# Attention scores of the first query block on one Trainium2 core: three f32r products in place of one f32 product

## The chip, the core and the metric

The kernel runs on one core of a Trainium2 chip. The metric is the device time of one execution in microseconds (us). Of the kernel before, three timed runs are known; a fourth execution was profiled. Engines are named as the profile names them: PE is TensorE (its matmuls), PEld is TensorE's weight loads, DVE is VectorE, ACT is ScalarE, POOL is GpSimd, SP is SyncE, which here only issues transfers.

## What is computed

Block-causal attention over 8 batches of 8 heads, 576 positions of 64 features, followed by a gated MLP over all 4608 tokens:

```python
scores = scale * np.matmul(q, k.transpose(0, 1, 3, 2))     # 576 x 576 for each of 64 heads
mask = block_i >= block_j                                   # blocks of 64 positions
scores = np.where(mask, scores, -1000000000.0)
...
attn = np.exp(scores)                                       # after the row maximum is taken off
attn = attn / (np.sum(attn, axis=-1, keepdims=True) + 1e-09)
return np.matmul(attn, v).astype(np.float32)
...
gate = 1.0 / (1.0 + np.exp(-(x @ w_gate)))
val = x @ w_val
return (gate * val @ w_out).astype(np.float32)
```

x is the attention's output with 512 features; w_gate and w_val are 512 x 1536, w_out is 1536 x 512.

## The kernel before

**Pairs.** Two heads make a pair, so there are 32 pairs. The 64 features of head 0 lie on partitions 0 to 63 and those of head 1 on partitions 64 to 127. KQ holds a pair's transposed keys (KQ[:, 0]) and queries (KQ[:, 1]), 576 columns each. The queries are cut into four blocks of 128 (block 0 to block 3) and a tail of 64; block i needs only the first 128(i+1) keys.

**Halves.** From pair 4 on (the constant REST_FROM), most score products are not taken from KQ itself. Keys and scaled queries are rounded to f32r (KH, QH) and what the rounding took off is rounded too (KL, QL). Three f32r products QH·KH, QL·KH and QH·KL add up to the score in PSUM. Five steps make the operands, in the function `prep_steps`: ACT writes KH ("ks", L395) and QH ("qs", L400), POOL writes KL ("kl", L405; DVE does it at L407 in the front), DVE writes QL ("ql", L409), and POOL copies the tail's queries into QBH and QBL ("qx", L415). A sixth step, "pm" (L402), has POOL multiply the 128 query columns of block 0 in KQ by the scale, in place: block 0 alone is still one f32 product of KQ with KQ, so it needs no halves, and QH and QL hold only the 448 columns behind it.

**Scores.** The function `scores` makes one block's products, for both heads. The two heads use different rows of PE's array (64 rows each, `tile_position`), so their matmuls run at the same time, and the profile shows them in twos. Block 3 has a PSUM tile of its own, block 2 too, and blocks 1 and 0 share one: block 1 in columns 0 to 255, block 0 in columns 256 to 383. In that third tile all three products of block 1 come first and the f32 product of block 0 stands last. An f32 matmul is two passes on PE, and the profile lists both.

**Order of the work.** Pairs 0 to 7 are laid out in a hand-written list (FRONT), which fixes the order of every instruction on every engine; this is the front, about the first 131 us. Pairs 8 to 31 run in a loop whose steps are listed in REST; between the steps the matmuls of the first third of the MLP (L179, L188) are dealt out to PE, so that PE has work while softmax and the transposes of other pairs run. On POOL a loop turn holds, in this order, DMA issues that move blocks of exponentials (L621), XL (L844), four copies into G (L615), the issue of rb (L292: the reciprocal sums, spread over the partitions), then pm and kl of the next pair, the issue of r_d (L292, it waits for rT of DVE at L568) and qx. The division L703 on DVE needs rb; it frees the PSUM tile that the scores of a later block are written to. From about 545 us on only the rest of the MLP runs (L1341, L1411).

Of the kernel before, what the change touches and what calls it, by code (L numbers as in the profile page):

```python
# [48 lines left out]
c2a.3@ rc.3 d2.c4 xh.1@ t3b.3 rD.3 pm.4 S10.4 t3a.3 c3b.3 tlb.3 x0.2 x1.2 dH.c3 S3.4 ms10.4@ c3a.3 tla.3 clb.3 pm.5  # L49
# [7 lines left out]
ldq.7 d4.o0 c3.5 h.10 tt5.5 h.11 tl.5 pm.6 ql.6 ldva.5@ d3.c7 h.12 cta.5 kl.6 ctb.5 ldq.8 d4.c7 t2.5 ldvb.5 dH.c6 cl.5  # L57
# [3 lines left out]
AV0.5 qs.7 gt.2 f.o2 st.4 AV1.5 ks.7 ext.6 d4.o1 c2.6 ldvb.7 ql.7 x0.5 sq.o2 ldvc.7 t3.6 h.23 d5.o1 ldvc.8 rc.6 pm.7  # L61
tl.6 kl.7 x1.5 ldq.9 qx.7 St.7 pa.o1 c3.6 dH.o1 cl.6 tt5.6 gm.2 gl.1@ dL.o1 dk.8 h.24 h.25 h.26 f.o3@ rD.6 cta.6 mxt.7
ext.7 d1.o2 d2.o2 ctb.6 ldva.8@ S2.7 S3.7 st.5 ms3.7@ ms2.7@ S10.7 d3.o2 d4.o2 d5.o2 gh.2 sq.o3 xl.4@ ldvb.8 h.27
mx2.7 gt.3 pm.8 h.28 pa.o2 h.29 h.30 ms10.7@ rB.6 dH.o2 gl.2 h.31 mx3.7 ldk.9 e2a.7 mx0.7 dL.o2 e2b.7 mx1.7 e3a.7 gm.3
# [9 lines left out]
def attn_glu_kernel(ctx: ExitStack, tc: tile.TileContext, q, k, v, w_gate, w_val, w_out, out):  # L74
    nc = tc.nc
# [152 lines left out]
    with ExitStack() as s2:  # L228
# [9 lines left out]
        KS, QS = [at.tile([P, S], F32R, name=f"K{e}") for e in "HL"], [at.tile([P, S - P], F32R, name=f"Q{e}") for e in "HL"]  # L238
# [99 lines left out]
        def mark(engine, ins):  # L338
            last[engine] = ins.ins
# [39 lines left out]
        def rows(h):  # L379
            return slice(64 * h, 64 * h + 64)  # L380

        def prep_steps(p):

            KQ = cv.tile([P, 2, S], F32, name="KQ", bufs=2)

            def step(what, alt=False):
                if what in ("dk", "dq"):
                    i = "kq".index(what[1])
                    turn = last.get("DVE")
                    ins = nc.vector.transpose(out=KQ[:, i], in_=rqks[p % 2][:, i])  # L390
                    for other in maxima or [turn] * bool(turn):
                        behind(ins.ins, other)
                    mark("DVE", pin("DVE", ins))
                elif what == "ks":
                    ins = nc.scalar.copy(out=KS[0], in_=KQ[:, 0])  # L395
                    for other in exps:
                        behind(ins.ins, other)
                    mark("ACT", pin("ACT", ins))
                elif what == "qs":
                    mark("ACT", pin("ACT", nc.scalar.mul(out=QS[0], in_=KQ[:, 1, P:], mul=scale)))  # L400
                elif what == "pm":
                    chain("POOL", pin("POOL", nc.gpsimd.tensor_scalar_mul(KQ[:, 1, :P], KQ[:, 1, :P], scale)))  # L402
                elif what == "kl":
                    if alt:
                        chain("POOL", pin("POOL", nc.gpsimd.tensor_sub(out=KS[1], in0=KQ[:, 0], in1=KS[0].bitcast(F32))))  # L405
                    else:
                        mark("DVE", pin("DVE", nc.vector.tensor_sub(out=KS[1], in0=KQ[:, 0], in1=KS[0].bitcast(F32))))  # L407
                elif what == "ql":
                    chain("DVE", pin("DVE", nc.vector.scalar_tensor_tensor(  # L409
                        out=QS[1], in0=KQ[:, 1, P:], scalar=scale, in1=QS[0].bitcast(F32), op0=ALU.mult,  # L410
                        op1=ALU.subtract)))
                elif what == "qx":
                    for x, src in zip(QBS, QS):
                        for h in range(2):
                            chain("POOL", pin("POOL", nc.gpsimd.tensor_copy(out=x[rows(h), h], in_=src[rows(h), S - P - D:])))  # L415
                state[p] = KQ, None, VSs[p % 3]

            return step

        def prep(p):  # L420

            step = prep_steps(p)
            for part in (("dk", "dq", "ks", "qs", "pm", "kl"), ("ql",), ("qx",)):
                for what in part:
                    step(what, what == "kl")
                yield

        def attend(p):
# [38 lines left out]
            def scores(ps, i, c):  # L467


                n = P * (i + 1)  # L470
                q = slice(i * P, (i + 1) * P)
                ops = [(KQ[:, 1, q], KQ[:, 0, :n])]
                if rest and i:
                    q = slice((i - 1) * P, i * P)
                    ops = [(QS[a][:, q], KS[b][:, :n]) for a, b in ((0, 0), (1, 0), (0, 1))]
                for k, (x, y) in enumerate(ops):
                    for h in range(2):
                        matmul(ps[:, h, c:c + n], lhsT=x[rows(h)], rhs=y[rows(h)], start=(k == 0),
                               stop=(k == len(ops) - 1), tile_position=(64 * h, 0))
                        if h == k == 0:  # L480
                            first_mm[:] = pe_last
# [21 lines left out]
            def s_blocks(*groups):  # L503
# [4 lines left out]
                for k, (ps, group) in enumerate(zip(tiles, groups)):  # L508
                    for j, i in enumerate(group):
                        scores(ps, i, 2 * P * j)  # L510
                        if rest and dealt and k == j == 0:
                            behind(first_mm[0], dealt[-1])
# [204 lines left out]
            def fine(what, alt=False, queue=nc.sync):  # L717

                i, h = what[1:2], "ab".find(what[-1])
                if what[0] == "S":  # L720
                    group = (1, 0) if i == "1" else () if i == "t" else (int(i),)
                    ps = keep["S" + i] = two_banks()
                    for j, c in enumerate(group):
                        scores(ps, c, 2 * P * j)
# [843 lines left out]
```

## Time and profile before

| | us |
|---|---|
| three timed runs | 1096.95, 1099.28, 1099.80 |
| their median | 1099.28 |
| the profiled execution, its own time | 1099.69 |
| span of the profiled execution | 1097.8 |

The span is the time from the first to the last recorded instruction on the core; the execution's own time also holds what lies around it (1.89 us). Instructions of a matmul overlap, since each is recorded until its last result is written: the distance from one start to the next says what one costs, its duration does not.

### The profile page before, as it was taken

The numbers are of one execution on the slowest core, as the hardware profiler recorded it, in microseconds if no ns is written. First come the engines' busy times: TensorE is split into PE (matmuls) and PEld (weight loads), VectorE is DVE, ScalarE is ACT, GpSimd is POOL, SyncE is SP. The second block draws the span as 40 slices with busy tenths as digits, with TensorE's granted clock in tenths as the row PEclk, the third lists the DMA queues.
The fourth block names the chain that finished last, engine by engine and source line by source line (L and its number), as shares of the span: only waits on it lengthen the run. The fifth ranks groups of instructions, "written<-read, shape, count | busy, mean of one in ns | idle before, by whom it ended". The sixth has DMA issues, their size and how long they took to land.

```text
span 1097.8 us, 19466 instructions
## 1 busy us (share of the span) xinstructions
PE 1080.7 (98%) x6593; PEld 929.5 (85%) x6593; DVE 862.1 (79%) x1488; ACT 602.7 (55%) x1321; POOL 532.3 (48%) x692
## 2 busy tenths in 40 slices
PE   8899999999999999999999999999999999999998
PEld 6577777778787778778899999999999999999997
DVE  6899999898989898787699768578785585665744
ACT  6887777777787777643353444534454142341421
POOL 3655499898989898710113030321305336243340
PEclk9999999999999999999999999999999999999999
DMA  8797599899888887745033362350886517345251
GB/s 162 162 206 159 128 184 190 187 189 197 185 194 177 200 175 184 198 122 170 22 97 103 123 221 78 144 187 34 293 296 230 188 50 224 103 128 186 74 164 58
DMA packets 264619, 174.87 MB, mean 159 GB/s; under 512 B 200988, under 2 KB 222092, under 8 KB 263880
## 3 DMA queue, kind: packets, MB, share of 16 engines
q1 hardware_dynamic: 247000, 148.54, 50.6%
q0 software_dynamic: 7008, 17.68, 6.9%
q10 hardware_dynamic: 10512, 7.41, 2.3%
q8 instruction: 52, 0.85, 0.3%
q14 instruction: 47, 0.39, 0.1%
HBM read 104.73 MB, written 47.60 MB: 139 GB/s over the span
## 4 chain that ended last, share of the span: by engine, by line
PE 83%; DVE 4%; DMA 4%; ACT 3%; POOL 2%; issue 2%; SPq 1%; ACTq 0%; DVEq 0%; POOLq 0%
PE b L1341 32%; PE m L1411 12%; PE bank L358 11%; PE m L179 10%; PE m L188 7%; PE b L1411 7%; PE bank L179 3%; SPq L292 1%; DMA rqk<-in_q_dram 1%; DMA rqk<-in_k_dram 1%; DMA rb<-r_d 1%; PE bank L188 1%; POOL G L615 1%; PE bank L363 1%; ACT XB L499 1%
## 5 line engine op out<-in xcount | busy, mean ns | idle before, releaser
L1341 PE MATMUL b<-XH,w 128*128 128x384 f32 x1344 | 349.0, 335 | 0.0
L1341 PEld LDWEIGHTS b<-XH,w 128*128 128x128 f32 x1344 | 243.8, 188 | 3.6
L1341 PE MATMUL b<-XL,w 128*128 128x384 f32 x672 | 223.5, 335 | 0.0
L1136 POOL TENSOR_TENSOR XB<-XB 128x384 f32<-128x384 f32 x20 | 21.5, 1076 | 238.0 <-DMA XB<-xT_d 238.0
L1341 PEld LDWEIGHTS b<-XL,w 128*128 128x128 f32 x672 | 126.1, 188 | 1.7
L1411 PE MATMUL m<-wo,hH 128*128 128x512 f32 x368 | 119.9, 391 | 0.0
L358 PE MATMUL bank<-G,VS 128*64 128x64 f32 (+3 forms) x1264 | 95.0, 305 | 2.6 <-POOL G L615 1.5
L358 PEld LDWEIGHTS bank<-G,VS 128*64 128x64 f32 x1264 | 64.6, 137 | 35.1 <-issue 7.6
L1364 ACT ACTIVATE g<-g 128x384 f32<-128x384 f32 x72 | 37.8, 525 | 93.1 <-DVE g L1377 49.3
L1149 ACT CAST XH<-XB 128x1536 fp32r<-128x1536 f32 (+2 forms) x72 | 65.1, 941 | 35.7 <-DVE XB L1147 27.3
L188 PE MATMUL m<-wo,hH 128*128 128x512 f32 x256 | 83.8, 393 | 0.0
L179 PE MATMUL m<-XH,wg 128*128 128x512 f32 x240 | 81.2, 394 | 0.4 <-ACT t L203 0.4
L179 PE MATMUL m<-XH,wv 128*128 128x512 f32 x240 | 81.2, 395 | 0.0
L1411 PEld LDWEIGHTS m<-wo,hH 128*128 128x128 f32 x368 | 69.0, 188 | 12.9
L487 DVE TENSOR_REDUCE nm<-bank 128x2 f32<-128x1024 f32 (+1 forms) x96 | 76.9, 801 | 2.2 <-ACT Z L499 0.6
L1150 DVE TENSOR_TENSOR XL<-XB,XH 128x1536 fp32r<-128x1536 f32 (+2 forms) x72 | 75.8, 1085 | 0.0
L1411 PE MATMUL m<-wo,hL 128*128 128x512 f32 x184 | 72.1, 392 | 0.0
L1411 PE MATMUL b<-wo,hH 128*128 128x512 f32 (+1 forms) x216 | 71.4, 383 | 0.0
L1405 POOL TENSOR_TENSOR pr<-pr,pr 128x512 f32<-128x512 f32 x33 | 42.6, 1296 | 42.6 <-DMA pr<-part_d 29.6
L499 ACT ACTIVATE Z<-bank,nm 128x512 f32<-128x512 f32 (+3 forms) x104 | 53.5, 529 | 7.8 <-DVE nm L487 4.5
L188 PEld LDWEIGHTS m<-wo,hH 128*128 128x128 f32 x256 | 47.9, 188 | 9.9 <-issue 0.2
L1349 POOL TENSOR_TENSOR hL<-v,hH 128x384 fp32r<-128x384 f32 x36 | 38.9, 1094 | 33.0 <-ACT hH L1348 30.3
(219 smaller groups left out, 2626.3 us busy)
## 6 DMA issues: line engine op xcount, KB each, us to landing
pr<-part_d SPq DMA_DIRECT2D x66, 256.0 KB
XB<-xT_d SPq DMA_DIRECT2D x16, 576.0 KB
part_d<-pr SPq DMA_DIRECT2D x36, 256.0 KB
rqk<-in_q_dram SPq DMA_DIRECT2D x120, 72.0 KB
rqk<-in_k_dram SPq DMA_DIRECT2D x120, 72.0 KB
out_dram<-pr SPq DMA_DIRECT2D x33, 256.0 KB
wgv_d<-st SPq DMA_DIRECT2D x8, 896.0 KB
w<-wgv_d SPq DMA_DIRECT2D x4, 1792.0 KB
```

The source lines that it names most:

```text
L179: mm = nc.tensor.matmul(ps, lhsT=lh, rhs=rh, start=(i == 0), stop=(i == n - 1))
L188: mm = nc.tensor.matmul(ps, lhsT=lh[:, f, t * P:(t + 1) * P], rhs=rh, start=(f == i == 0), stop=(f == F1 - 1 and i == 2))
L358: pe_last[:] = [pin("PE", nc.tensor.matmul(*args, **kw)).ins]
L487: mark("DVE", nc.vector.tensor_reduce(out=nm_()[:, c0:c0 + 2], in_=ps[:, :, c:c + n], axis=AX.X, op=ALU.max, negate=True))
L499: mark("ACT", nc.scalar.activation(out=dst, in_=src, func=AF.Exp, bias=nm_()[:, c0 + h:c0 + h + 1], accum_out=sm[:, 5 * h + i:5 * h + i + 1]))
L1149: nc.scalar.copy(out=XO[j][0][:, a:b], in_=x)
L1150: sub = nc.vector.tensor_sub(out=XO[j][1][:, a:b], in0=x, in1=XO[j][0][:, a:b].bitcast(F32))
L1341: mm = nc.tensor.matmul(ps, lhsT=lh, rhs=rh, start=(first and k == 0), stop=(k == n - 1), skip_group_check=not first)
L1349: (nc.vector if q else nc.gpsimd).tensor_sub(out=hL[:, f, n:n + N2], in0=h, in1=hH[:, f, n:n + N2].bitcast(F32))
L1364: mark2("ACT", nc.scalar.activation(out=t, in_=c, func=AF.Tanh, scale=0.5))
L1405: nc.gpsimd.tensor_add(out=pr[t], in0=pr[t], in1=other)
L1411: mm = nc.tensor.matmul(po[t][:, cols], lhsT=lh[:, f, t * P:(t + 1) * P], rhs=wo[:, f, e, cols], start=((whole or half == 0) and i == 0), ...
```

## The change

Block 0 is now made from the halves like the other blocks. QH and QL have 576 columns (448 before), so "qs" on ACT and "ql" on DVE run over all queries; "pm" is gone from POOL, in the loop and five times from the front's list. `scores` takes several blocks and goes through them product by product: QH·KH of block 1, QH·KH of block 0, QL·KH of block 1, QL·KH of block 0, and so on. Only block 1's first product opens the PSUM bank (`start`).

```diff
-c2a.3@ rc.3 d2.c4 xh.1@ t3b.3 rD.3 pm.4 S10.4 t3a.3 c3b.3 tlb.3 x0.2 x1.2 dH.c3 S3.4 ms10.4@ c3a.3 tla.3 clb.3 pm.5
+c2a.3@ rc.3 d2.c4 xh.1@ t3b.3 rD.3 S10.4 t3a.3 c3b.3 tlb.3 x0.2 x1.2 dH.c3 S3.4 ms10.4@ c3a.3 tla.3 clb.3 
...
-        KS, QS = [at.tile([P, S], F32R, name=f"K{e}") for e in "HL"], [at.tile([P, S - P], F32R, name=f"Q{e}") for e in "HL"]
+        KS, QS = [at.tile([P, S], F32R, name=f"K{e}") for e in "HL"], [at.tile([P, S], F32R, name=f"Q{e}") for e in "HL"]
...
-                    mark("ACT", pin("ACT", nc.scalar.mul(out=QS[0], in_=KQ[:, 1, P:], mul=scale)))
-                elif what == "pm":
-                    chain("POOL", pin("POOL", nc.gpsimd.tensor_scalar_mul(KQ[:, 1, :P], KQ[:, 1, :P], scale)))
+                    mark("ACT", pin("ACT", nc.scalar.mul(out=QS[0], in_=KQ[:, 1], mul=scale)))
...
-                        out=QS[1], in0=KQ[:, 1, P:], scalar=scale, in1=QS[0].bitcast(F32), op0=ALU.mult,
+                        out=QS[1], in0=KQ[:, 1], scalar=scale, in1=QS[0].bitcast(F32), op0=ALU.mult,
...
-            for part in (("dk", "dq", "ks", "qs", "pm", "kl"), ("ql",), ("qx",)):
+            for part in (("dk", "dq", "ks", "qs", "kl"), ("ql",), ("qx",)):
...
-            def scores(ps, i, c):
...
+            def scores(ps, *blocks):
+
+                todo = []
+                for i, c in blocks:
+                    n = P * (i + 1)
+                    q = slice(i * P, (i + 1) * P)
+                    ops = [(QS[a][:, q], KS[b][:, :n]) for a, b in ((0, 0), (1, 0), (0, 1))] if rest else \
+                        [(KQ[:, 1, q], KQ[:, 0, :n])]
+                    todo.append([(x, y, c, n, k == 0, k == len(ops) - 1) for k, (x, y) in enumerate(ops)])
+                for k, step in enumerate(zip(*todo)):
+                    for j, (x, y, c, n, start, stop) in enumerate(step):
+                        for h in range(2):
+                            matmul(ps[:, h, c:c + n], lhsT=x[rows(h)], rhs=y[rows(h)], start=start and j == 0, stop=stop,
+                                   tile_position=(64 * h, 0), skip_group_check=j > 0)
```

PE's instructions at the scores of one pair of the loop, from block 2's last product to the MLP's next matmul, stand before as follows (x2 is one for each head; the f32 product of KQ is one row here and two passes on PE):

```order
L358 MATMUL bank<-KL,QH 128x384 x2
L358 MATMUL bank<-KH,QH 128x256 x2
L358 MATMUL bank<-KH,QL 128x256 x2
L358 MATMUL bank<-KL,QH 128x256 x2
L358 MATMUL bank<-KQ 128x128 x2
L179 MATMUL m<-XL_435,wv_117 128x512
```

With the change the same place reads:

```order
L358 MATMUL bank<-KL,QH 128x384 x2
L358 MATMUL bank<-KH,QH 128x256 x2
L358 MATMUL bank<-KH,QH 128x128 x2
L358 MATMUL bank<-KH,QL 128x256 x2
L358 MATMUL bank<-KH,QL 128x128 x2
L358 MATMUL bank<-KL,QH 128x256 x2
L358 MATMUL bank<-KL,QH 128x128 x2
L179 MATMUL m<-XL_435,wv_117 128x512
```

The f32 product is gone, and a product of 128 columns stands behind each of block 1's; nothing else moved on PE here.

POOL's instructions of one loop turn, from the last issue of rb to the tail's copies, stand before as follows:

```order
L292 DMA rb<-r_d 64x512
L218 TENSOR_TENSOR hL<-h_2055,hH 128x512
L402 TENSOR_SCALAR KQ<-KQ 128x128
L405 TENSOR_TENSOR KL<-KQ,KH 128x576
L292 DMA r_d<-rT 4x32x32
L415 COPY QBH<-QH 64x64 x2
```

With the change (lines behind 402 are two lower):

```order
L292 DMA rb<-r_d 64x512
L218 TENSOR_TENSOR hL<-h_2079,hH 128x512
L403 TENSOR_TENSOR KL<-KQ,KH 128x576
L292 DMA r_d<-rT 4x32x32
L413 COPY QBH<-QH 64x64 x2
```

The scaling of KQ is gone from ahead of KL; the rest of the turn keeps its order.

## Rows read from the trace of the kernel before

**Rows 1.** The page's first part: busy us (share of the span) xinstructions.

```profile
span 1097.8 us, 19466 instructions
...
PE 1080.7 (98%) x6593; PEld 929.5 (85%) x6593; DVE 862.1 (79%) x1488; ACT 602.7 (55%) x1321; POOL 532.3 (48%) x692
```

**Rows 2.** Busy us by stretch: us, engines (xinstructions), granted clock, DMA share, GB/s.

```profile
50.00:100.00 50.00, 47.21 (x336) 35.62 (x335) 47.41 (x88) 42.74 (x111) 28.79 (x34) 1.00 0.83 182
...
200.00:250.00 50.00, 49.88 (x400) 39.65 (x400) 44.41 (x77) 37.64 (x90) 45.66 (x71) 1.00 0.93 186
...
350.00:400.00 50.00, 48.95 (x354) 39.04 (x354) 43.32 (x73) 38.60 (x100) 44.30 (x68) 1.00 0.87 191
```

**Rows 3.** Longest waits of PE, 131 to 545 us: us in total, times, longest us.

```profile
PE bank L358 <- DVE xT L703: 2.1, 5, 0.8
PE bank L358 <- POOL G L615: 1.5, 1, 1.5
PE bank L358 <- DVE QL L409: 0.7, 2, 0.4
```

**Rows 4.** PE in order of time, pair 15's blocks 1 and 0: start us, us, instruction.

```profile
218.47 0.38 PE L358 MATMUL bank<-KH,QH 64*128 64x256 f32 x2
218.66 0.31 PE L358 MATMUL bank<-KH,QL 64*128 64x256 f32 x2
218.78 0.31 PE L358 MATMUL bank<-KL,QH 64*128 64x256 f32 x2
218.90 0.41 PE L358 MATMUL bank<-KQ 64*128 64x128 f32 x4
219.24 0.50 PE L179 MATMUL m<-XL,wv 128*128 128x512 f32 x1
```

**Rows 5.** The same, from 219.20 us on: the second pass of KQ alone.

```profile
219.00 0.31 PE L358 MATMUL bank<-KQ 64*128 64x128 f32 x2
```

**Rows 6.** Weight loads of the same place, in order of time.

```profile
218.44 0.21 PEld L358 LDWEIGHTS bank<-KH,QH 64*128 64x128 f32 x2 [0.34 <-PE bank L358]
218.54 0.22 PEld L358 LDWEIGHTS bank<-KH,QL 64*128 64x128 f32 x2
```

**Rows 7.** PE in order of time in the front: f32r products, then another array layout.

```profile
54.24 0.33 PE L358 MATMUL bank<-KH,QL 64*128 64x384 f32 x2
54.41 0.34 PE L358 MATMUL bank<-KL,QH 64*128 64x384 f32 x2
54.68 0.44 PE L363 MATMUL m<-ident,Z 128*128 128x128 f32 x2
```

**Rows 8.** Line L402 (pm): count, duration ns min/median/max, first and last start.

```profile
L402 POOL TENSOR_SCALAR KQ<-KQ x28: 523/524/1185, 48.2 to 443.5; 128x128 f32<-128x128 f32 x28
```

**Rows 9.** POOL in order of time, pair 12's pm and kl.

```profile
172.15 0.52 POOL L402 TENSOR_SCALAR KQ<-KQ 128x128 f32<-128x128 f32 x1
172.67 1.40 POOL L405 TENSOR_TENSOR KL<-KQ,KH 128x576 fp32r<-128x576 f32 x1
```

**Rows 10.** DVE in order of time, pairs 11 (from 158 us) and 12 (from 173 us).

```profile
158.19 1.43 DVE L565 TENSOR_SCALAR sm<-sm 128x9 f32<-128x9 f32 x1
...
160.04 0.58 DVE L409 SCALAR_TENSOR_TENSOR QL<-KQ,QH 128x448 fp32r<-128x448 f32 x1
...
173.09 1.46 DVE L409 SCALAR_TENSOR_TENSOR QL<-KQ,QH 128x448 fp32r<-128x448 f32 x1
```

**Rows 11.** PE in order of time, its waits in pairs 11 to 13 and 27.

```profile
160.68 0.50 PE L358 MATMUL bank<-KH,QL 64*128 64x512 f32 x2 [0.26 <-DVE QL L409]
...
174.61 0.50 PE L358 MATMUL bank<-KH,QL 64*128 64x512 f32 x2 [0.44 <-DVE QL L409]
...
189.89 0.39 PE L358 MATMUL bank<-KH,QH 64*128 64x256 f32 x2 [0.35 <-DVE xT L703]
...
391.39 0.39 PE L358 MATMUL bank<-KH,QH 64*128 64x256 f32 x2 [0.27 <-DVE xT L703]
```

**Rows 12.** ACT in order of time, pair 11's QH.

```profile
157.39 0.60 ACT L400 ACTIVATE QH<-KQ 128x448 fp32r<-128x448 f32 x1
```

More of the change, by code (lines that the diff above doesn't have):

```diff
@@ L56 @@
 st.3 d4.c6 d1.c7 e0b.5 d3.o0 ks.6 d5.c6 AV0.4 pa.c6 e0a.5 AV1.4 ldva.7 x0.4 e1a.5 x1.4 gm.0 d2.c7 t3.5 qs.6 sq.c7
-ldq.7 d4.o0 c3.5 h.10 tt5.5 h.11 tl.5 pm.6 ql.6 ldva.5@ d3.c7 h.12 cta.5 kl.6 ctb.5 ldq.8 d4.c7 t2.5 ldvb.5 dH.c6 cl.5
+ldq.7 d4.o0 c3.5 h.10 tt5.5 h.11 tl.5 ql.6 ldva.5@ d3.c7 h.12 cta.5 kl.6 ctb.5 ldq.8 d4.c7 t2.5 ldvb.5 dH.c6 cl.5
 h.13 rc.5 gt.1 c2.5 d5.c7 qx.6 d5.o0 S2.6 pa.c7@ ms2.6@ rD.5 mx2.6 S3.6 sq.o1 S10.6 ms3.6@ h.14 dH.c7 h.15 xh.4
@@ L60 @@
 h.19 mx0.6 dL.o0@ d1.o1 rB.5 dk.7 e1b.6 gh.1 e3a.6 h.20 d2.o1 h.21 h.22 e1a.6 St.6 ldk.8 d3.o1 e0a.6 t2.6 e0b.6 mxt.6
-AV0.5 qs.7 gt.2 f.o2 st.4 AV1.5 ks.7 ext.6 d4.o1 c2.6 ldvb.7 ql.7 x0.5 sq.o2 ldvc.7 t3.6 h.23 d5.o1 ldvc.8 rc.6 pm.7
+AV0.5 qs.7 gt.2 f.o2 st.4 AV1.5 ks.7 ext.6 d4.o1 c2.6 ldvb.7 ql.7 x0.5 sq.o2 ldvc.7 t3.6 h.23 d5.o1 ldvc.8 rc.6
 tl.6 kl.7 x1.5 ldq.9 qx.7 St.7 pa.o1 c3.6 dH.o1 cl.6 tt5.6 gm.2 gl.1@ dL.o1 dk.8 h.24 h.25 h.26 f.o3@ rD.6 cta.6 mxt.7
 ext.7 d1.o2 d2.o2 ctb.6 ldva.8@ S2.7 S3.7 st.5 ms3.7@ ms2.7@ S10.7 d3.o2 d4.o2 d5.o2 gh.2 sq.o3 xl.4@ ldvb.8 h.27
-mx2.7 gt.3 pm.8 h.28 pa.o2 h.29 h.30 ms10.7@ rB.6 dH.o2 gl.2 h.31 mx3.7 ldk.9 e2a.7 mx0.7 dL.o2 e2b.7 mx1.7 e3a.7 gm.3
+mx2.7 gt.3 h.28 pa.o2 h.29 h.30 ms10.7@ rB.6 dH.o2 gl.2 h.31 mx3.7 ldk.9 e2a.7 mx0.7 dL.o2 e2b.7 mx1.7 e3a.7 gm.3
 e0b.7 d1.o3 d2.o3 xh.5 e1b.7 e3b.7 e1a.7 d3.o3 u.0 e0a.7 AV0.6 d4.o3 d5.o3 ldq.10 ldk.10 AV1.6 rc.7 ks.8 tt5.7 pa.o3@
@@ L414, in step @@
                         for h in range(2):
-                            chain("POOL", pin("POOL", nc.gpsimd.tensor_copy(out=x[rows(h), h], in_=src[rows(h), S - P - D:])))
+                            chain("POOL", pin("POOL", nc.gpsimd.tensor_copy(out=x[rows(h), h], in_=src[rows(h), S - D:])))
                 state[p] = KQ, None, VSs[p % 3]
@@ L465, in copy_out @@
                     mark("ACT", pin("ACT", nc.scalar.copy(out=dst, in_=src)))
-            def scores(ps, i, c):
[L470 to L481, printed above, removed]
+            def scores(ps, *blocks):
[11 more added lines that the diff above has]
+                                   tile_position=(64 * h, 0), skip_group_check=j > 0)
+                            if h == k == j == 0:
+                                first_mm[:] = pe_last
             def softmax(ps, i, c):
@@ L508, in s_blocks @@
                 for k, (ps, group) in enumerate(zip(tiles, groups)):
[L509 to L512, printed above, removed]
+                    scores(ps, *((i, 2 * P * j) for j, i in enumerate(group)))
+                    if rest and dealt and k == 0:
+                        behind(first_mm[0], dealt[-1])
                 if rest:
@@ L722, in fine @@
                     ps = keep["S" + i] = two_banks()
-                    for j, c in enumerate(group):
-                        scores(ps, c, 2 * P * j)
+                    if group:
+                        scores(ps, *((c, 2 * P * j) for j, c in enumerate(group)))
                     if not group:
```

## The prediction, made before the changed kernel was run

> **What bounds the kernel now.** I read the page's first part, then busy time by stretch, then PE's waits, then single places in order of time. In the first part PE is busy for 1080.7 of 1097.8 us [rows 1]. The stretches say where it is not the whole story: at 50 to 100 us PE idles 2.8 of 50 us while DVE is busy for 47.4; at 200 to 250 us it idles 0.12; at 350 to 400 us, 1.05, with POOL busy for 44.3 [rows 2]. [...] The waits behind the front give the names: 2.1 us in five places for xT (the division that frees a PSUM tile), 1.5 us once for a POOL copy into G, 0.7 us in two places for QL [rows 3]. So a pair of the loop costs what PE has to do, plus a few short waits on a chain in which POOL and DVE take turns. The change touches both: it gives PE more matmuls, and takes work from POOL.
>
> **PE's part.** The place to read is pair 15, blocks 1 and 0 [rows 4]. [...] The f32 product of block 0 starts at 218.90 and the MLP's next matmul at 219.24, 0.34 us. Its two passes start 0.10 us apart (218.90, 219.00 [rows 4, 5]), and 0.24 us go from the second pass to the MLP's first matmul, which uses the whole array again.
>
> After the change the steps behind block 1's three products stay what they are (0.19, 0.12, 0.12), since each is set by block 1's own columns. New are the step from block 0's product to block 1's next, x, twice, and the step from block 0's last product to the MLP, y. A pair's change is 2x + y - 0.34.
>
> For x no row shows an f32r product of 128 columns. [...] From above: such a product takes as long as the f32 one, two passes of 0.10, x = 0.20. What stands nearest is the weight load. Where block 1's matmul has to wait for it, two loads of 128 columns start 0.10 us apart (218.44, 218.54 [rows 6]), and the next load starts when a matmul starts, not earlier. Weights for 128 columns of output are loaded for every product, whatever it streams, so a short product gives the next load no more than its own start. I take x = 0.105. The interleaving thus hides block 0's own loads behind 256 columns and leaves block 1's loads in the open.
>
> [...]
>
> For y: in the front an f32r product of 384 columns is followed by another layout after 0.27 us, and two such products stand 0.17 apart [rows 7]. With 256 columns fewer, at 0.05 for 128, y = 0.16. If nothing is won against the f32 pass, y = 0.24. The two heads do not start together in this place, which the first row does not have, so I take 0.19.
>
> So a pair costs 2 x 0.105 + 0.19 - 0.34 = +0.06 us on PE, and the 28 pairs from 4 to 31 cost **+1.7 us**. The bounds are 2 x 0.06 + 0.16 - 0.34 = -0.06 (**-1.7 us**) and 2 x 0.20 + (0.24 + 0.10) - 0.34 = +0.40 (**+11.2 us**).
>
> **POOL's part.** pm is gone 28 times, 0.52 us each in the loop and up to 1.19 in the front [rows 8]. KL stands right behind it, so in the turns in which POOL is the late one, KL starts and ends 0.52 us earlier. What that is worth is seen at QL. In pair 12 KL runs from 172.67 to 174.07 [rows 9]; QL starts on DVE at 173.09 and takes 1.46 us, to 174.55 [rows 10], where undisturbed it takes 0.58 (pair 11 [rows 10]). It ends 0.48 us behind KL. In pair 11 even an addition on 9 columns, L565, takes 1.43 us. DVE stands still there while POOL works through KL.
>
> [...]
>
> In pair 12, KL would end at 173.55 and QL 0.48 + 0.17 later, at 174.20 instead of 174.55: 0.35 us less of the 0.44 that PE waits for it [rows 11]. (0.17 is QL's price for 128 more columns, 0.58 x 128 / 448.) PE's next wait is for xT, which DVE does behind QL; it moves along with QL and gives nothing more. In pair 11, L565 and QL come 0.52 earlier and QL 0.17 longer: the wait of 0.26 goes. At 189.89 and 391.39 PE waits 0.35 and 0.27 us for xT, whose rb POOL issues; in both places POOL has worked without a pause since a pm, so rb comes 0.52 earlier and both waits go. Together 0.35 + 0.26 + 0.35 + 0.27 = **-1.2 us**. The other waits (two for xT, the 1.5 us for G) I leave: there POOL had waited for others between pm and the late step. Bounds: nothing is won (0), or all of rows 3 goes (-4.3 us).
>
> **DVE and ACT.** QL grows by 0.17 us, QH by at most 0.60 x 128 / 448 = 0.17 [rows 12], 28 times: 4.8 us on each. At 200 to 250 us DVE idles 5.6 us in 50 and ACT 12.4 [rows 2], some 1.6 and 3.5 us for a pair's turn of about 14.4 us. That idle time is the cover, and I count both at nothing beyond the 0.17 above; with the cover gone it is up to 4.8 us. Queued behind QL on DVE are the divisions L703, for which PE waits; this is where it would show.
>
> **The front** has four of the pairs and five pm. PE's extra work there lies in its idle 2.8 us [rows 2]; DVE, nearly full, gets 4 x 0.17 and is freed of five blocks by pm. I count zero, give or take 0.7.
>
> **Sum.** 1.7 - 1.2 = +0.5 us. The profiled execution took 1099.69, which gives 1100.2; it lay 0.41 above the median of the runs shown, so I forecast a median of **1099.8**. The runs before spread from 1096.95 to 1099.80; 0.3%, 3.3 us, is about what this kernel's measurement can tell from no change, so this is no change.
>
> **The rivals.**
>
> *Dear products (slower).* An f32r product of 128 columns doesn't run at one column per cycle but takes as long as f32. Place: the six short products of every pair. Price: +11.2 - 1.2 = +10.0, **1109.3**. For it: no row has an f32r product below 256 columns, and two f32 passes and the loads all show 0.10, so rows do not separate streaming from loading. Against it: 256, 384 and 512 columns follow one line with their number of columns. It decides from x and y together 0.16 us per pair above now (28 x 0.16 = 4.5 = 3.3 + 1.2), that is from x of about 0.14.
>
> *A full DVE (slower).* QL's growth is not covered in the loop and POOL's relief reaches no wait, since KL waits for KH instead: 1.7 + half of 4.8 = +4.1, **1103.4**. For it: DVE is busy for 44.4 of 50 us where PE is the bound and 47.4 in the front. Against it: part of that busy time is waiting for POOL, which shrinks.
>
> *POOL was the bound (faster).* The relief of 28 x 0.52 = 14.7 us on POOL takes all of rows 3, 4.3 us, and the short products come at their lower bound, -1.7: -6.0, **1093.3**; with PE's +1.7 it would be -2.6, 1096.7, which is no change. For it: POOL busy for 45.7 of 50 us. Against it: PE idles 0.12 us there, so in most turns POOL's delay reaches nobody.
>
> **How the numbers follow.** The forecast gets 0.61, its own range is 1097.3 to 1102.3 (±2.5: the runs' own spread, ±0.02 on x, half of the waits). Dear products 0.09, a full DVE 0.15, POOL the bound 0.15. Slower is dear products, two thirds of the full DVE and 0.03 of the forecast: 0.22. Faster is two thirds of POOL's case and 0.02 of the forecast: 0.12. The rest, 0.66, is no change. The range goes down to 1096.2, which takes in POOL's case with PE's price, and up to 1103.8, past the full DVE; outside are the dear products, the upper part of the full DVE and the gain's end, about 0.2.
>
> **What would show it.** Right: in the changed profile block 0's products are followed by block 1's next after 0.10 to 0.11 us, the MLP's matmul comes 0.16 to 0.20 behind the last, PE's waits for QL at pairs 11 and 12 are gone or under 0.2, and QL undisturbed takes about 0.75. Wrong: steps of 0.2 us behind products of 128 columns; new waits of PE for QL or xT; a front that ends elsewhere than at about 131 us by more than a microsecond; or waits behind POOL's G that vanish, which I have not counted.

## The result and the profile after

The changed kernel takes **1109.91 us** (median of 6 runs, 1106.80 to 1114.71); the kernel before, in the same rounds, 1099.49 (6 runs). The ratio is **1.0098**, 95% interval 1.0069 to 1.0127: slower by 1%, outside the forecast's range. A second batch of runs gave the same ratio, 1.0098 (1.0080 to 1.0117). In the changed kernel most lines behind L402 are two lower than before, some one: KL is L403, QL L407, xT L701, the copies into G are L613 on POOL and L463 on ACT.

The page's first part answers to [rows 1]:

```profile
span 1109.7 us, 19526 instructions
...
PE 1083.5 (98%) x6649; PEld 932.7 (84%) x6649; DVE 870.1 (78%) x1488; ACT 605.2 (55%) x1321; POOL 514.3 (46%) x664
```

The span grew by 11.9 us, PE's busy time by 2.8 only. So PE waits more; the change's own matmuls are not where most of the time went. PE in order of time at pair 15's blocks 1 and 0, the place of [rows 4]:

```profile
220.70 0.45 PE L358 MATMUL bank<-KH,QH 64*128 64x256 f32 x4 [1.26 <-DVE xT L701]
220.95 0.42 PE L358 MATMUL bank<-KH,QL 64*128 64x256 f32 x4
221.18 0.42 PE L358 MATMUL bank<-KL,QH 64*128 64x256 f32 x4
221.53 0.50 PE L179 MATMUL m<-XL,wv 128*128 128x512 f32 x1
```

x4 is two heads by two blocks. From the first product to the MLP's matmul it is 0.83 us, against 0.77 in [rows 4]: +0.06, as forecast. The wait in the first row is the news. PE's waits from 131 to 557 us, which answer to [rows 3]:

```profile
PE bank L358 <- DVE xT L701: 4.9, 4, 2.7
PE bank L358 <- ACT G L463: 4.0, 1, 4.0
PE bank L358 <- POOL G L613: 1.5, 1, 1.5
PE bank L358 <- POOL hL L218: 1.4, 1, 1.4
PE bank L358 <- DVE QL L407: 0.6, 1, 0.6
```

xT costs 2.8 us more than before. The ACT copy into G (4.0 us) and hL (1.4 us) are single waits in the last pair. In the front there is one more, 1.6 us for xT near 55 us. Where the span grew is read from when a place of the program is reached. Pair 31's first score product starts 4.64 us later than before (453.34, before 448.70), the first matmul of the rest of the MLP 11.27 us later (556.86, before 545.59), the end 11.86 us later. So pairs and front lost 4.6 us, **the tail between pair 31's scores and the rest of the MLP lost 6.6**, the rest 0.6. These are the parts of one execution. In a second profile of the changed kernel (the run "changed again" below) they are 2.9, 8.2 and 0.4 us. The front makes the difference: pair 8's first score product starts at 121.51 us in the first profile, at 119.96 in the second, and at 119.96 before. The first profile also has a stretch at half clock there (granted clock 0.66 from 31 to 36 us, 1.00 before).

What happens in the tail begins on SP's queue. The queue of the changed kernel in order of time (start us, us):

```profile
449.70 0.89 SPq L1067 DMA_DIRECT2D raw<-in_moe_w_gate_dram  x2
450.68 0.96 SPq L1127 DMA_DIRECT2D XB<-xT_d  x2
451.75 3.28 SPq L619 DMA_DIRECT2D G<-Z  x5
```

The same queue of the kernel before:

```profile
444.95 3.17 SPq L621 DMA_DIRECT2D G<-Z  x5
...
451.88 0.98 SPq L1069 DMA_DIRECT2D raw<-in_moe_w_gate_dram  x2
```

raw in these rows is the second early fetch for the rest of the MLP. It is written to a buffer that it shares with KQ (the pool's tag KQ has two buffers). Before, the last reader of pair 31's KQ was block 0's f32 product on PE, and the scheduler put raw behind the moves G<-Z of pair 30. Now KQ's last readers are KL and QL. The buffer comes free earlier in the program, so the scheduler put raw ahead of the moves. But raw then stands at the head of SP's queue, with the moves behind it, and waits for these two, on POOL (first row) and DVE:

```profile
447.61 1.41 POOL L403 TENSOR_TENSOR KL<-KQ,KH 128x576 fp32r<-128x576 f32 x1
```

```profile
448.11 1.52 DVE L407 SCALAR_TENSOR_TENSOR QL<-KQ,QH 128x576 fp32r<-128x576 f32 x1
```

QL ends at 449.63 and raw is issued at 449.70. The moves, which were issued at 444.95 before, come 6.8 us later. Some 4.1 us of this the program was late already: the transpose of Z on DVE, after which they can go, ends at 447.63, before at 443.48. The other 2.7 are the place behind raw. The moves read Z, and pair 31's exponentials are written to Z, so ACT waits:

```profile
459.54 0.69 ACT L498 ACTIVATE Z<-bank,nm 128x512 f32<-128x512 f32 x1 [5.53 <-DMA G<-Z]
```

The landing is late too. POOL issues four of the moves itself, at 449.71, while raw and XB go out on SP. From issue to landing, POOL's moves around this turn take, in the changed kernel (first row) and before:

```profile
DMA to landing us min/median/max: 3.1/4.1/7.9
DMA to landing us min/median/max: 2.4/3.4/4.2
```

That raw and XB are under way at the same time is a likely reason, but no run separates it from the place on the queue.

The scheduler moved more near the end: on ACT also t and XH, on DVE two steps of an early fetch, on SP rb and XL. Those stay where the change put them in the kernel with both orders restored (below), whose tail is back at 97.0 us. One more counts, on ACT. Before, the cast hH<-h (L214) stood behind the last two copies G<-bank of the last pair:

```profile
464.87 1.53 ACT L465 COPY G<-bank 128x768 f32<-128x768 f32 x3 [0.47 <-PE bank L363]
468.16 0.62 ACT L214 CAST hH<-h 128x512 fp32r<-128x512 f32 x1 [1.76 <-DVE h L207]
```

Now it stands ahead of them. It waits 2.76 us for DVE's h, and the copies wait behind it:

```profile
474.99 0.62 ACT L214 CAST hH<-h 128x512 fp32r<-128x512 f32 x1 [2.76 <-DVE h L207]
475.52 0.75 ACT L463 COPY G<-bank 128x512 f32<-128x512 f32 x2
```

PE needs these copies and waits 3.98 us for them:

```profile
476.15 3.24 PE L358 MATMUL bank<-G,VS 128*64 128x320 f32 x12 [3.98 <-ACT G L463]
```

The same 12 products took 1.83 us before:

```profile
466.28 1.83 PE L358 MATMUL bank<-G,VS 128*64 128x320 f32 x12 [0.45 <-ACT G L465]
```

The stretch's row says why (us, engines, granted clock behind POOL's):

```profile
475.60:479.00 3.40, 2.85 (x12) 1.24 (x12) 0.69 (x1) 0.66 (x3) 0.00 (x0) 0.50 1.06 241
```

Late in PE's idle time its granted clock fell to 0.50 (1.00 from 475.3 to 475.6 us) and stayed there for 3.4 us.

That is no single case. The profiled execution has two such stretches, this one and the one behind 31 us (0.50 from 32 to 35 us), and a mean granted clock of 0.997; that of the kernel before has none, and 1.000. By these numbers one stretch alone, 3.4 us at 0.50 in 1100, makes a mean of 0.998 (an estimate). Of 128 executions of the kernel before beside the variants 98 have a mean of 1.000 (one slow execution, 1783 us at 0.557 throughout, is left out); of the 12 of the changed kernel none has, they lie between 0.992 and 0.998. So part of the loss is paid in clock.

### The profile page after: what moved, and what is told of

Read it like the earlier page. It is cut to its first block, busy times and chain, and to the rows that moved or that the text cites. A ratio compares the mean times of both kernels' runs of the same rounds, so it can differ in the third digit from the quotient of the medians.

```text
span 1109.7 us, 19526 instructions
## 1 busy us (share of the span) xinstructions
PE 1083.5 (98%) x6649; PEld 932.7 (84%) x6649; DVE 870.1 (78%) x1488; ACT 605.2 (55%) x1321; POOL 514.3 (46%) x664
## 4 chain that ended last, share of the span: by engine, by line
PE 52%; DVE 4%; issue 1%; DMA 1%; ACT 1%; DVEq 0%
PE b L1339 29%; PE m L1409 11%; PE b L1409 6%; PE bank L179 3%; PE m L188 1%; PE m L179 1%; DMA raw<-in_moe_w_out_dram 1%; PE bank L188 0%; DVE XL L1148 0%; PE bank L358 0%; DVE raw L1062 0%; ACT Z L498 0%; DVE XB L1137 0%; DVE cT L1058 0%; DVE cT L1063 0%
```

## The experiments

The times are ratios to the kernel before, measured beside it on the same chip, with the 95% interval; 0.001 is 1.1 us. "Tail" is, in the profiled execution, the time from pair 31's first score product to the first matmul of the rest of the MLP: 96.9 us before, 103.5 in the changed kernel.

### The tail

**SP's order restored.** The second early fetch is held behind pair 30's moves:

```diff
                     behind(d.ins, last2["SP"])
                 else:
+                    if len(early) == 1:
+                        behind(d.ins, last["moves"])
                     mark2("SP", d)
```

> The changed kernel, with one order added: the second early fetch for the rest of the MLP (raw twice, XB twice) stays behind the moves of pair 30 on SP's queue, as it stood before the change. Queue theory: in the changed kernel raw heads the queue and waits for the last reader of a KQ tile until 449.70, so the moves G<-Z are issued at 451.75 instead of 444.95, and the last pair's exponentials wait 5.53 us for them. Then this run gains 6 to 7 us on the changed kernel (about 1103.2, or 3.7 over before), the exponentials of pair 31 start behind their maxima, and the waits of 1.43 and 3.98 us on PE behind them are gone. Rival, dear products or a fuller DVE in every pair: the tail is not the place, and the time stays within 1.5 us of the changed kernel's 1109.9.

Measured: 1.0038 (1.0025 to 1.0052), 1104.41 us. By the ratios 6.6 us of the loss are back, the exponentials start behind their maxima again and PE's wait of 1.43 us for hL is gone. The wait for the G copy is shorter (2.71 us) but still there, and that part of what I expected failed: it has another cause. The rival falls, since no pair was touched.

**ACT's cast, in three programs.** The first restores SP's order and holds the cast behind the copies ("G" is set to pair 31's last copy):

```diff
-            pin("ACT", nc.scalar.copy(out=hH, in_=got[1]))
+            ins = pin("ACT", nc.scalar.copy(out=hH, in_=got[1]))
+            if not scripted and "G" in last:
+                behind(ins.ins, last.pop("G"))
```

> The changed kernel with two orders restored in the last pair: the early fetch behind the moves on SP, as in the run with the tail's order restored, and on ACT the cast hH<-h behind the last two copies out of the transposes (G<-bank), where it stood before the change. Theory of the cast: the cast waits for DVE's h (a wait of 2.76 us in the changed kernel), the two copies stand behind it and PE waits for them (3.98 us there, 2.71 us with only SP's order restored); so this run gains another 4 us, from 1104.4 to about 1100.4, and what is left over before is the pairs' own (PE's 1.7 us and stalls of rb). Rival, the rounding of 576 columns is what costs (the run with the wide rounding alone was 5.2 us slower than before): it stays within 1.5 us of 1104.4.

The second is the kernel before with this one cast moved ahead of the last two copies; all other instructions keep their order on every engine:

> The kernel before with nothing changed but the place of one ACT instruction in the last pair: the cast hH<-h ahead of the last two copies G<-bank, as the changed kernel has it. Theory of the cast: 3 to 4.5 us slower than before (1102 to 1103.5), with a PE wait of some 3 us for a G copy near 470. Rival, the order is a symptom and the lateness comes from elsewhere: no difference over 1 us.

The third is the changed kernel again:

> The changed kernel once more, on the chip and in the rounds of the three others, as their yardstick. If the losses that its profile shows belong to the program, they are there again: the wait of ACT's exponentials for G<-Z (5.5 us) and PE's wait for a G copy (4 us) in the last pair, each within 1 us. The waits of 1.26 us and 2.66 us for xT in pairs 15 and 26 come back if they belong to the program, and stand elsewhere or are shorter if they are chance. Time 1107 to 1112.

Measured: the kernel before with the cast moved, 1.0033 (1.0019 to 1.0047): one instruction's place costs 3.6 us, and its tail is 101.5 us. Its trace has ACT in order of time as the changed kernel has it:

```profile
465.52 0.62 ACT L214 CAST hH<-h 128x512 fp32r<-128x512 f32 x1 [2.53 <-DVE h L207]
466.05 0.75 ACT L467 COPY G<-bank 128x512 f32<-128x512 f32 x2
```

The changed kernel again: 1.0098, with the same waits in the tail (3.98 us for the G copy, 1.85 us in front of pair 31's tail scores) and the waits of 1.39 and 2.06 us for xT in pairs 15 and 26 at the same places; the losses belong to the program.

With both orders restored: 1.0039 (1.0021 to 1.0058). The tail is back at 97.0 us, yet the ratio is that of SP's order alone, 1.0038, and not 4 us less as I expected. The two had run on different chips, and so the three variants were run once more, on one chip.

**The two orders apart.** The changed kernel with the cast alone restored, with SP's order alone, and with both:

> The changed kernel with ACT's order restored in the last pair (the cast hH<-h behind the two copies G<-bank) and SP's left as the change made it. If the two losses are separate and add up: 3 to 4.5 us faster than the changed kernel, ratio to before 1.006 to 1.007, and the exponentials of the last pair still wait 5.5 us for G<-Z. If SP's order is the cause of both (late exponentials make the copies late whatever ACT's order): no gain, 1.009 to 1.010.

> The changed kernel with SP's order alone restored, as in the first experiment, beside the other two on one chip. By the first time of it: ratio 1.0038; by its profile (the ACT loss of 4 us is still there, and the waits of the pairs) 1.006.

> Both orders restored, beside the two runs with one of them. If the losses add up: 3 to 4 us faster than the run with SP's order alone of this call (ratio about 1.0035). If ACT's order is worth nothing once SP's is restored: equal to it within 1 us.

| changed kernel with | ratio | tail in the profile, us |
|---|---|---|
| neither order restored | 1.0098 (1.0080 to 1.0117), 1.0098 (1.0069 to 1.0127) | 105.1, 103.5 |
| ACT's cast restored | 1.0050 (1.0033 to 1.0068) | 101.6 |
| SP's order restored | 1.0052 (1.0033 to 1.0072), 1.0038 (1.0025 to 1.0052) | 98.9, 100.9 |
| both restored | 1.0035 (1.0019 to 1.0051), 1.0039 (1.0021 to 1.0058) | 97.1, 97.0 |
| kernel before | 1 | 96.9 |

By the ratios each alone gives 5 to 6.6 us back, both 6.5 to 6.9, so they overlap. That one late instruction partly hides the other, as both delay the same chain of exponentials, transposes and copies, would explain it, but is not shown. The profiles speak less for it: the second repair is worth 0 to 1.9 us by the times, but 1.8 to 4.5 us by the tail. Single tails also differ by what the 12 products behind the G copy take: SP's order alone has 100.9 us where they take 3.44 us (mean granted clock of that execution 0.995) and 98.9 where they take 1.84 (1.00 from 450 to 475 us). So my "separate and add up" is not decided. With SP's order left as it is, the last pair's exponentials still wait for G<-Z (6.9 us; I expected 5.5). What is left with both restored, 3.8 to 4.3 us, lies ahead of the tail.

### The load on DVE and ACT

**Wide rounding alone.** The kernel before with QH and QL of 576 columns. Block 0 keeps its f32 product, of a query that POOL scales into an unused tile instead of in place:

```diff
-chain("POOL", pin("POOL", nc.gpsimd.tensor_scalar_mul(KQ[:, 1, :P], KQ[:, 1, :P], scale)))
+chain("POOL", pin("POOL", nc.gpsimd.tensor_scalar_mul(
+    QBs[p % 2].rearrange("p h d -> p (h d)"), KQ[:, 1, :P], scale)))
...
-        out=QS[1], in0=KQ[:, 1, P:], scalar=scale, in1=QS[0].bitcast(F32), op0=ALU.mult,
+        out=QS[1], in0=KQ[:, 1], scalar=scale, in1=QS[0].bitcast(F32), op0=ALU.mult,
...
```

> The kernel before, with QH and QL of 576 columns (ACT and DVE 0.1 to 0.17 us longer per pair) and nothing else: block 0's scores are still f32 products of a scaled query, which POOL scales into another tile instead of in place. If the longer roundings lie under cover, as I forecast: within 1 us of before. If DVE is full: 3 to 5 us slower than before.

Measured: 1.0047 (1.0034 to 1.0059), 5.2 us, what I had expected of a full DVE or a little more. Taken alone it would have been a wrong verdict: its tail is 101.5 us, because the scheduler had put the cast ahead of the copies here too. The same program with the cast held behind them:

> The run with the wide rounding alone, with the one cast hH<-h behind the two copies G<-bank again, as before. Theory of the cast: it gives back the 4.6 us that that run lost between the scores of the last pair and the rest of the MLP, so 1104.9 becomes about 1100.3, within 1.5 us of before. Rival, DVE and ACT are full: it stays 4 to 5 us over before, since each of the 28 pairs still rounds 576 columns.

Measured: 1.0021 (1.0009 to 1.0033), tail 97.0 us. So 2.9 of its 5.2 us were the cast's place, and **the wide roundings cost about 2.3 us** (1.0 to 3.6), not nothing and not 4.8. POOL's scaling into another tile is part of that price, and the trace shows no one place for it: from pair 8's first score product to pair 31's it takes 329.2 us, before 328.7; most of the rest lies in the front, which differs as much between profiles of one program (121.51 and 119.96 above).

### The order of the short products

**Not interleaved.** SP's order restored, block 1's three products first and then block 0's three:

```diff
-                for k, step in enumerate(zip(*todo)):
-                    for j, (x, y, c, n, start, stop) in enumerate(step):
+                for j, block in enumerate(todo):
+                    for k, (x, y, c, n, start, stop) in enumerate(block):
```

> As the run with the tail's order restored, but the three products of block 1 stand first and the three of block 0 behind them, so that a weight load of a 128-column product lies beside another 128-column product only. If the weight load sets the pace of short products (about 0.105 us each, two per step), block 0's three steps take 0.21 us each instead of the 0.13 that they add when interleaved: +0.08 x 3 = +0.23 us in each of 28 pairs, up to +6.4 us. If the streaming of columns sets it, there is no difference (under 0.5 us).

Measured: 1.0052 (1.0037 to 1.0067), beside 1.0038 on the same chip and 1.0052 on the other for the interleaved one: no difference that these times resolve. The rows of PE at pair 18, where it does not wait, tell more:

```profile
261.76 0.28 PE L358 MATMUL bank<-KH,QH 64*128 64x256 f32 x2
...
262.11 0.22 PE L358 MATMUL bank<-KH,QH 64*128 64x128 f32 x2
262.17 0.28 PE L358 MATMUL bank<-KH,QL 64*128 64x128 f32 x2
262.29 0.27 PE L358 MATMUL bank<-KL,QH 64*128 64x128 f32 x2
262.49 0.50 PE L179 MATMUL m<-XL,wg 128*128 128x512 f32 x1
```

From the first short product to the second it is 0.06 us, half of the 0.12 from block 1's first product of 256 columns to its second (261.76, 261.88); from the second to the third 0.12. Each of these two starts 0.06 to 0.07 us behind the start of its own weight load, and the loads start 0.11 apart (262.00, 262.11 and 262.22, for both heads at once). Together 262.49 - 261.76 = 0.73 us; interleaved (SP's order restored, the same pair) it is 262.37 - 261.65 = 0.72, in the kernel before 261.94 - 261.27 = 0.67. So the third short product came at the pace of the loads here, but the order of the products made no difference in the sum. My upper end (+6.4 us) came from counting the loads of the two heads one behind the other.

### POOL's freed time

**POOL's load kept in the loop.** SP's order restored; POOL still scales 128 columns at pm's place in the loop, as mere work:

```diff
+elif what == "pm":
+    chain("POOL", pin("POOL", nc.gpsimd.tensor_scalar_mul(
+        QBs[p % 2].rearrange("p h d -> p (h d)"), KQ[:, 1, :P], scale)))
```

> As the run with the tail's order restored, but POOL still does the old scaling of 128 columns (0.52 us, at its old place ahead of KL, into a tile that nobody reads) in the pairs of the loop, not in the five that the front list deals out. If POOL's relief is worth nothing: within 1 us of that run. If it was worth the 1.2 us that I forecast, or more: slower by 1.2 to 4.3 us. If KL standing directly behind the issue of rb is what makes rb land late (6.44 and 6.83 us after issue in pairs 15 and 26, against 5.16 and 4.90 before): faster by some 2.5 us, since those waits of xT go.

Measured: 1.0032 (1.0020 to 1.0045). In this program the scheduler left the cast behind the copies by itself (tail 96.9 us), so it compares with both orders restored, 1.0035 and 1.0039, not with SP's alone: no difference that these times resolve. The gain of 2.5 us did not come.

**POOL's load kept everywhere.** Both orders restored, and pm's work also at its five places in the front's list:

> The changed kernel with the last pair's two orders restored and with POOL's old scaling of 128 columns kept as mere work (into a tile nobody reads) at all its old places, those of the front list too. What is left of the change is its three short products and the wider roundings. Theory that POOL's relief hurts: in the front POOL's XL then starts behind DVE's rT again, DVE's small operations are short again (0.16 us instead of 1.23, 0.65 instead of 1.33), PE's wait of 1.6 us near 54 is gone, and so is that near 219; with PE's 1.7 us and the wide roundings (2.3 us in their own run) the time is 1099.5 to 1102. Rival, the relief is neutral: 1103, as with both orders alone, and the wait near 54 stays.

Measured: 1.0021 (1.0010 to 1.0032), 1.5 to 2 us faster than without that work, with intervals that overlap. The wait near 54 us is gone; that near 219, which I expected to go too, is still there (0.72 us). The first one's cause is read in the changed kernel, DVE first, then POOL:

```profile
51.50 1.24 DVE L563 TENSOR_SCALAR sm<-sm 128x9 f32<-128x9 f32 x1
52.77 0.22 DVE L564 RECIPROCAL sm<-sm 128x9 f32<-128x9 f32 x1
53.02 0.21 DVE L566 STREAM_TRANSPOSE rT<-sm 128x32 f32<-128x32 f32 x1
53.16 1.33 DVE L155 SCALAR_TENSOR_TENSOR cgv<-cgv 128x512 uint32<-128x512 uint32 x1
54.41 0.81 DVE L807 TENSOR_TENSOR xT<-bank,rb 128x256 f32<-128x256 f32 x2
```

```profile
51.29 1.41 POOL L818 TENSOR_TENSOR XL<-xT,XH 128x576 fp32r<-128x576 f32 x1
52.67 1.27 POOL L169 TENSOR_TENSOR wv<-cgv,wv 128x512 fp32r<-128x512 f32 x1
```

And with POOL's load kept:

```profile
49.02 0.16 DVE L568 TENSOR_SCALAR sm<-sm 128x9 f32<-128x9 f32 x1
...
49.60 0.65 DVE L155 SCALAR_TENSOR_TENSOR cgv<-cgv 128x512 uint32<-128x512 uint32 x1
```

```profile
49.08 0.51 POOL L418 CAST QBL<-QL 64x64 fp32r<-64x64 f32 x2
49.68 1.85 POOL L825 TENSOR_TENSOR XL<-xT,XH 128x576 fp32r<-128x576 f32 x1
```

With pm on POOL, XL starts when DVE is through with rT (49.68) and is itself the one that takes longer (1.85 us instead of 1.41). Without it, XL starts ahead of DVE's addition on 9 columns, which then takes 1.24 us instead of 0.16; L155 stands beside POOL's next operation (1.33 us instead of 0.65). xT is 1.6 us late, and PE waits. The wait stands in the trace of every program whose front lacks pm (1.06 to 1.62 us) and in none whose front has it. What the rows show of the reason: L563 ends with XL (52.74 and 52.70 us) and L155 0.55 us behind POOL's next operation (54.49 and 53.94), while L564 and L566, in between, take the same 0.22 and 0.21 us in both profiles. Why the one takes longer beside the other is not shown.

### The waits for rb in the loop

In pair 26 the trace of the changed kernel, asked for rb, shows that the transfer lands late:

```profile
L292 POOL DMA_DIRECT2D rb<-r_d x3: 524/526/541, 373.0 to 374.0; - x3
...
DMA to landing us min/median/max: 4.0/4.6/5.8
```

Before, the same three issues stood at 370.5 to 371.6 and landed after 3.7/3.8/3.9 us. **rb first**: POOL issues rb ahead of its four copies, which take 3.5 us, in the kernel with both orders restored, in the kernel before, and in the one with POOL's load kept everywhere:

```diff
-REST = (... ("mc", 0), ("rb", 0), ("t", 4), ...)
+REST = (... ("rb", 0), ("mc", 0), ("t", 4), ...)
```

> The changed kernel with the last pair's two orders restored, and POOL issues rb ahead of its four copies G<-Z in each pair of the loop, not behind them, 3.5 us earlier. If the waits of xT near 219 and 379 (1.3 and 2.1 to 2.7 us) come from rb's landing, as the profile shows, they are gone and the run gains 2 to 3.5 us on the 1103.1 of both orders alone. The copies end 1.57 us later; between their end and the product that reads G there were 0.9 to 4.3 us, so at two or three pairs up to 0.7 us may be lost. Rival, rb only stands for something else that is late (the bank's product, DVE): no gain, within 1 us of 1103.

> The kernel before with POOL's issue of rb ahead of the four copies G<-Z in each pair of the loop. Its own waits for xT are 0.35, 0.47 and 0.78 us in the profile: a gain of 0.5 to 1.5 us (1097), if the later copies cost nothing; between 0 and 1 us slower if they do.

> The run with POOL's load kept everywhere and rb ahead of the copies, both: if rb's landing is what POOL's load moves in the loop, the two gains are not added up there, and this run is within 1 us of the better of the two, at 1099 to 1101. If they are separate causes, it is 1 to 2 us faster than either, and beats the changed kernel by 10 us; against the kernel before it is then PE's 1.7 us slower (1099.7) or a little less.

Measured: the changed one 1.0006 (0.9995 to 1.0016), 3.2 to 3.6 us faster than without; the waits for xT in its loop are down to 0.2 us. The kernel before 1.0015 (1.0006 to 1.0024): slower. Other steps now come late, which would account for it: in its trace PE waits 3.0 us for a copy into G near 445 (1.5 before) and 1.2 us for a transfer G<-Z near 147. With POOL's load 1.0009 (0.9996 to 1.0022): once rb is early, the times show no gain from POOL's load, although the wait near 54 us is gone in this trace too.

**XL last.** To spare the copies, XL was put behind them in the kernel before (order rb, copies, XL):

> The kernel before with POOL's order in the loop rb, copies G<-Z, XL (it was XL, copies, rb; in the turn of pair 30 copies, rb, XL), and with the cast hH<-h held behind the copies G<-bank of the last pair. Theory: rb lands 5 us earlier, so the waits for xT (0.35, 0.47, 0.78 us) go, the copies stay where they were but in the turn of pair 30, where they end 1.4 us earlier and the wait of 1.49 us near 442 shrinks: 2 to 3 us faster than before (ratio 0.997 to 0.998). [...]

Measured: 1.0034 (1.0022 to 1.0046), a miss. XL is needed sooner than I thought: PE waits 2.0 us for it at 371, and 2.5 us for h at 451.

**rb first where it pays.** In all turns but those of pairs 9 and 30, behind which the plain swap had made PE wait:

```diff
+                if p not in (N_FIRST + 2, n - 2) and what in ("rb", "mc"):
+                    what = "mc" if what == "rb" else "rb"
```

> The kernel before with rb issued ahead of the copies G<-Z on POOL in all turns of the loop except those of pairs 9 and 30, where the plain swap cost 1.2 and 1.5 us. It was 1.0015 with the plain swap; 2.5 us less is 0.999 to 1.000: the waits for xT go (1.6 us in the profile), one copy near 373 is late (0.67 us).

> The changed kernel with both orders of the last pair restored and the same selection. With the plain swap it was 1.0006; without its two late copies (0.55 and 1.45 us) 0.9985 to 0.999 if the pairs cost only what PE's row says; the wait of 1.6 us near 54 is still there. If the wide roundings and POOL's freed time cost more than the waits for rb show, it stays at 1.001 to 1.003, 1 to 3 us behind the kernel before with the same selection.

Measured: the kernel before 0.9988 (0.9975 to 1.0001), 1098.28 us; the changed kernel, with both orders restored, **0.9998 (0.9980 to 1.0016)**, 1098.69 us. PE's waits from 118 to 545 us in the latter:

```profile
PE bank L360 <- POOL G L615: 2.0, 2, 1.4
PE bank L360 <- ACT G L465: 0.6, 1, 0.6
PE bank L360 <- DVE QL L409: 0.5, 1, 0.5
PE bank L360 <- DVE xT L705: 0.2, 1, 0.2
```

The 10 us are gone with three edits that only order instructions. Neither version is measurably faster than the kernel before; the kernel before with rb moved comes nearest (its interval just reaches 1).

## Why the prediction was wrong

**The step that failed is the sum itself, "1.7 - 1.2 = +0.5 us": it has no term for instructions that the scheduler moves on SP and ACT.** The sum follows the change on PE, POOL, DVE and ACT within a pair. But the change also takes away KQ's last reader on PE, and with it goes the order of one transfer and one cast in the last pair. Of the 10.8 us by which the ratio says the changed kernel is slower, 6.5 to 6.9 go with these two. That four transfers had changed places on SP could be known before the run, as the orders on PE and POOL were; the prediction names none of them and gives them no price. That the places themselves cost the time is shown by the restored orders and, for the cast, by the kernel before with it moved.

That 1109.91 lies beside the price of the dear products, 1109.3, is chance, as the steps below show.

**PE, +1.7 us: right in its sum, by two errors that cancel.** The change costs +0.06 us at pair 15 and +0.05 at pair 18 (0.72 after 0.67), 28 times 1.4 to 1.7 us. But x is not 0.105. Block 0's three products at pair 15, one by one:

```profile
220.89 0.26 PE L358 MATMUL bank<-KH,QH 64*128 64x128 f32 x2
221.12 0.25 PE L358 MATMUL bank<-KH,QL 64*128 64x128 f32 x2
221.35 0.25 PE L358 MATMUL bank<-KL,QH 64*128 64x128 f32 x2
```

Block 1's stand at 220.70, 220.95 and 221.18, the MLP's matmul at 221.53 (the rows at the top merge the blocks). So a short product is followed by block 1's next after 0.06 us, which is x at its lower bound. No row of the kernel before shows that 0.06; what its rows show is 0.05 us for 128 columns more, 256 columns in 0.12 [rows 4] and 384 in 0.17 [rows 7]. Block 1's second and third steps, which I took to stay at 0.12, are 0.17: twice 0.045 less and twice 0.05 more. y is 0.18, near its 0.19. What held is the pace of the weight loads, 0.11 to 0.12 us apart (220.77, 220.89, 221.00, 221.12, 221.23); that the next load starts only when a matmul starts did not (221.00 and 221.23 have none beside them). The dear products fall: not one step near 0.2 us stands behind a short product, except where the array's layout changes. (Their threshold is x = 0.155 with y = 0.19, not 0.14.)

**POOL, -1.2 us: wrong in its sum, by the waits that it left alone.** Of the four waits that it counts three went: the QL wait of pair 11 and those for xT in pairs 13 and 27. That of pair 12 stayed, 0.57 us after 0.44, but not by a long QL. KL, now earlier, starts ahead of the addition on 9 columns on DVE, which ends with it (174.17 and 174.15 us) and takes 1.31 us, 0.40 before; QL stands behind it and takes 0.72 us, near the 0.75 that I had forecast:

```profile
172.72 1.43 POOL L403 TENSOR_TENSOR KL<-KQ,KH 128x576 fp32r<-128x576 f32 x1
```

```profile
172.86 1.31 DVE L563 TENSOR_SCALAR sm<-sm 128x9 f32<-128x9 f32 x1
...
175.05 0.72 DVE L407 SCALAR_TENSOR_TENSOR QL<-KQ,QH 128x576 fp32r<-128x576 f32 x1
```

The waits for xT outside the four grew: 1.26 us at pair 15, where there was none, 2.66 after 0.78 at pair 26, 4.9 in all with the others. Kept as mere work, POOL's scaling cost nothing in the loop that the times resolve, and in the front a wait of 1.6 us was gone with it. Less work on an engine was here not less delay.

**The front, 0 +- 0.7: not settled.** The wait of 1.6 us is new, and 0.5 us more stands near 100. But the front ends 1.6 us late in one profile of the changed kernel and not late in the other.

**DVE and ACT at nothing: mis-sized**, 2.3 us in its own run. That is what the full-DVE rival put on it (half of 4.8). The 3.8 to 4.3 us that are left with both orders restored are that rival's +4.1 in number, but not by its mechanism alone: 3.2 to 3.6 of them go when rb is issued earlier.

**What stays open.** Why rb lands later in the changed kernel. It is issued at the same place behind the copies, it lands 5.8 us later instead of 3.9 in pair 26, and it comes back at that pair in every variant that leaves rb behind the copies. PE's wait for xT there is 0.8 us before and 1.15 in the kernel before with the cast moved, 1.0 and 1.3 with the wide roundings alone, and 1.5 to 2.7 in all ten profiles with the short products, with POOL's load kept too (2.04 us). So the larger share came with the short products and what goes with them, not with the roundings alone or with POOL's freed time; the traces don't say how. That its landing is what PE waits for is shown by moving its issue. Nor do the times resolve PE's 1.7 us: the two repaired kernels differ by 0.0010, about 1.1 us, within their intervals.

## What to carry to other kernels

Where a scheduler orders the queues, compare the order on every engine before costing anything, transfers and casts included, and read each moved row as a wait: what does it wait for, and who stands behind it? A tile that loses its last reader frees its buffer earlier, and the next user of that buffer may move ahead of something that matters. And before an edit's price is believed, look whether the same program moved something else: one cast made "wide rounding" look twice as dear as it is.

## What the runs showed of the hardware

- PE's granted clock fell to 0.50 at the end of a wait: in the changed kernel from 475.6 to 479.0 us, at the end of 3.98 us of idling, where 12 products then took 3.24 us instead of 1.83. With SP's order alone restored the same products took 3.44 us behind 2.71 us of idling in one execution and 1.84 us behind 2.42 us in another. A wait of 2.06 us for xT in pair 26 (both orders restored, second run) went with a mean granted clock of 1.000 in that execution. In the kernel with both orders restored, 6 executions with a mean granted clock of 1.000 take 1101.4 us on average, 13 with 0.998 take 1103.6.
- An f32r product of 128 columns was followed by the next after 0.06 us, while the weight loads of 128 columns started 0.11 to 0.12 us apart: in pair 18 without interleaving it was 0.12 us from the second short product to the third, in pair 15 0.23 for one of 256 and one of 128 columns together.
- A DVE operation on 9 columns took 1.24 us where POOL's XL had started 0.21 us before it (the changed kernel, 51.50 us), and 0.16 where XL started behind it (POOL's load kept everywhere, 49.02 us).
